# Rows turned by TensorE's transpose path, logits from stationary gate weights

## The chip, the cores and the metric

One core of one Trainium2 chip. The metric is the device time of one execution in microseconds (us). Of the kernel before there are three timed executions and one profiled one.

## The reference, cut to what matters

A block-wise linear attention (64-row blocks, decay `lam` per head) is followed by a mixture-of-experts layer in which each token goes to one expert.

```python
# q, k, v: (4, 8, 768, 64); attention output (B,H,S,D) -> x: (3072, 512)
x = attn_out.transpose(0, 2, 1, 3).reshape(B * S, H * D)
logits = x @ w_gate                      # (3072, 512) @ (512, 8)
expert_idx = np.argmax(logits, axis=1)
probs = softmax(logits)                  # gate_w = probs of the chosen expert
for e in range(8):
    mask = expert_idx == e
    h = np.maximum(x[mask] @ w1[e], 0.0) # w1: (8, 512, 1024)
    out[mask] = gate_w[mask, None] * (h @ w2[e])   # w2: (8, 1024, 512)
```

All data is fp32.

## The kernel before, in words

**Attention stage.** The work is cut into 12 steps (`order`): six blocks of 128 positions times two pairs of batches. A step is a struct `m` (`begin`). In the main loop, iteration i handles `cur` (step i), prepares `ahead` (step i+1), and finishes `last` (step i-1). TensorE, VectorE, ScalarE and SyncE follow the order in which the code is written. In an iteration TensorE does, in this order:

- the rows of `last` (`leave` calls `rows`): its attention output, which stands feature-major in SBUF (`xT`), is turned to token-major and multiplied by the gate weights;
- the turns of `ahead` (`turn_q`, `turn_k`: `tq`, `tk`, 16 transposes of 128x128);
- `attend_states(cur, 0)`: products with the running state, in 64x64 quadrants of the array (`op`, L306);
- `grow`: the state update (`cp`, L335); `attend` (`op`, L318); `attend_states(cur, 1)`; for every second step `put` (the `rank` products);
- `score(ahead)` (`sp`, L282), in two row halves of the array.

ScalarE copies what stands in PSUM: from `rows` the logits (`lg`, L364) and the rows (`x`, L366), then `qT`, `kT`, the exponential `ex`, a one-column copy `fence` (L314), and at the end of the iteration `xT` (L327). `fence` reads the last column that `attend_states(cur, 0)` wrote, and `attend` writes the same bank, so TensorE's L318 waits for `fence`. Since each engine works its queue in order, `fence` waits for whatever ScalarE has before it, `ex` included. `ex` waits for VectorE's `sh`.

VectorE multiplies scores by the decay (`mt`), makes `qsT` out of `tq` behind ScalarE's `qT`, and runs `choose` (argmax and one-hot: `mx`, `sh`, `key`, `pick`, `oh`, `ohc`). `choose` runs once per group of four batches, that is in iterations 2, 4, 6, 8 and 10, and for the last block once per pair (iteration 11 and after the loop).

In the kernel before, each turn in `rows` is a plain fp32 matmul: the moving operand `back` holds, per pair of 128-feature chunks, the identity and the gate columns side by side, 136 columns, so one product gives turned rows and logits at once. Odd chunks stand with their 64-feature halves exchanged (`out_at`), and `back` undoes that.

SyncE's queue holds, per iteration, the store of the last step's rows to DRAM (`store_rows`, `xs`) and the three loads of step i+3 (`load`: q, k, v, each 512 KB in 256-byte pieces). GpSimd scales k (`kd`) and scatters routing entries (`slots`).

**Expert stage.** `hidden(zero)`, `outputs`, then seven passes with a Strassen-like scheme (`form`, L689 and L711) over gathered tokens. `load_first` and `load_second` bring an expert's weights.

PSUM has eight banks, given by number: `tq`/`tk`/`sp` use 0 to 3, `cp` 4, `rank` 5, `op` 6 and 7, and the four `tx` tiles 4 to 7.

Of the kernel before, what the change touches and what calls it, by code (L numbers as in the profile page):

```python
# [22 lines left out]
def kernel(  # L23
# [99 lines left out]
    W = P + E  # L123
    back = const.tile([P, DC // 2, 2 * W], F32, name="back")
    for c in range(DC // 2):
        nc.gpsimd.tensor_copy(back[:, c, :P], ident)
        nc.gpsimd.tensor_copy(back[:, c, P + 2 * E:W + E + D], ident[:, D:])
        nc.gpsimd.tensor_copy(back[:, c, W + E + D:], ident[:, :D])
    by_chunk = moe_w_gate.rearrange("(c j u d) e -> j u d c e", c=DC // 2, j=2, u=2)
    for j, u in itertools.product(range(2), range(2)):  # L130
        nc.gpsimd.dma_start(out=back[(u ^ j) * D:((u ^ j) + 1) * D, :, P + j * E:P + (j + 1) * E],
                            in_=by_chunk[j, u])
# [54 lines left out]
    def load_first(e):  # L187
        w1t = wpool.tile([P, DC, F], F32, tag="w1", name="w1t")
        nc.sync.dma_start(out=w1t, in_=pick(w1_r, e))
        return w1t  # L190
# [19 lines left out]


# [112 lines left out]
    def to_sbuf(m):  # L324
        for b in range(2):
            xT = work.tile([P, DC, C], F32, tag="xT", name="xT")
            nc.scalar.copy(xT, m.op[b])  # L327
            m.xT.append(xT)
# [21 lines left out]
    def rows(m, b, lg):  # L350

        if b == 0:
            m.x = row_pair("x")
        x = m.x[:, b]
        tx = [bank(4 + 2 * b + c, [P, 2, W], f"tx{c}") for c in range(DC // 2)]
        for c, t in enumerate(tx):
            flat = t.rearrange("p j w -> p (j w)")
            nc.tensor.matmul(flat[:, :W], lhsT=m.xT[b][:, 2 * c, :], rhs=back[:, c, :W],  # L358
                                 start=True, stop=False, skip_group_check=True)
            nc.tensor.matmul(flat[:, P:P + W], lhsT=m.xT[b][:, 2 * c + 1, :],  # L360
                                 rhs=back[:, c, W:], start=False, stop=True,
                                 skip_group_check=True)
        for c, t in enumerate(tx):
            nc.scalar.copy(lg[:, c, :], t[:, 0, P:])  # L364

            nc.scalar.copy(x.rearrange("p (a d f) -> p d a f", a=P // Q, d=DC)[:, 2 * c:2 * c + 2],  # L366
                           t[:, :, :P].rearrange("p d (a f) -> p d a f", f=Q))
# [5 lines left out]
    def choose(n, bs, lg):  # L373
        nb = len(bs)
        shp = [P, nb, E]
        parts, lg = lg, small.tile(shp, F32, tag="lg_sum", name="lg_sum")
        nc.vector.tensor_add(lg, parts[:, :, 0], parts[:, :, 1])
# [35 lines left out]
    def put(n, bs, oh, ohc, sh):  # L413
# [4 lines left out]
        rank = bank(5, shp, "rank")  # L418
# [230 lines left out]
    def token_sums(m):  # L649
        b = [[m.xgT[:, j * DH:(j + 1) * DH, k, m.off[k]:m.off[k] + m.h] for k in range(2)] for j in range(2)]  # L650
        t1, t2, t4 = (work.tile([P, DH, m.h], F32, tag=t, name=f"t_{t}", bufs=n)
                      for t, n in (("sd", 2), ("xT", 2), ("kd", 2)))

        m.b = right_sums(b, t1, t2, b[0][1], t4, nc.vector.tensor_sub)
# [205 lines left out]
    def leave(m):  # L860
        for b in range(2):
            n, bs = group_of[m.n, m.b + b]
            i = bs.index(m.b + b)
            if i == 0:
                lgs[0] = small.tile([P, len(bs), DC // 2, E], F32, tag="lg", name="lg")
            rows(m, b, lgs[0][:, i])
        store_rows(m)
        if i == len(bs) - 1:
# [54 lines left out]
    with tc.manual_schedule(engines={mybir.EngineType.PE, mybir.EngineType.DVE,  # L923
# [9 lines left out]
        for i in range(len(order)):  # L933
# [8 lines left out]
            new = leave(last) if last else None  # L942
# [6 lines left out]
            else:  # L949
                later_decays()  # L950
            if new:
# [23 lines left out]
            if ahead:  # L975
                for s in range(2):
# [4 lines left out]
                  1)  # L981
# [121 lines left out]
```

## Time and profile before

| | us |
|---|---|
| median of 3 runs | 442.14 (441.17 to 448.15) |
| profiled execution, its own time | 445.17 |
| span of the profiled execution | 443.3 |
| TensorE matmul busy in the span | 424.9 (96%) |
| VectorE / ScalarE / GpSimd busy | 265.7 / 152.7 / 120.5 |

The mean granted TensorE clock was 0.991 of full speed. The attention stage takes roughly the first 131 us; the rest is the expert stage. In the rows below, PE is TensorE's matmuls, PEld its weight loads, DVE VectorE, ACT ScalarE, POOL GpSimd, SP SyncE. An fp32 matmul leaves two records (two passes), a transpose one, so "x2" at `tx` is one product and "x4" at `tq` four transposes.

### The profile page before, as it was taken

The numbers are of one execution on the slowest core, as the hardware profiler recorded it, in microseconds if no ns is written. First come the engines' busy times: TensorE is split into PE (matmuls) and PEld (weight loads), VectorE is DVE, ScalarE is ACT, GpSimd is POOL, SyncE is SP. The second block draws the span as 40 slices with busy tenths as digits, with TensorE's granted clock in tenths as the row PEclk, the third lists the DMA queues.
The fourth block names the chain that finished last, engine by engine and source line by source line (L and its number), as shares of the span: only waits on it lengthen the run. The fifth ranks groups of instructions, "written<-read, shape, count | busy, mean of one in ns | idle before, by whom it ended". The sixth has DMA issues, their size and how long they took to land.

```text
span 443.3 us, 9039 instructions
## 1 busy us (share of the span) xinstructions
PE 424.9 (96%) x3575; PEld 397.9 (90%) x3575; DVE 265.7 (60%) x567; ACT 152.7 (34%) x370; POOL 120.5 (27%) x140
## 2 busy tenths in 40 slices
PE   3999999989999999999999999999999999999993
PEld 3989999889888569999999999999999999999772
DVE  2846556555654146784688289479749839937411
ACT  2355544534561110441144135224414413413411
POOL 6425373605062540052104200600500200200121
PEclk9999999989999999999999999999999999999997
DMA  9999999999986989779979859947977966605012
GB/s 176 240 227 239 205 202 196 204 208 195 291 230 160 295 234 370 226 197 362 261 211 375 230 134 325 327 96 242 355 185 187 356 193 148 229 24 125 27 59 73
DMA packets 128208, 95.52 MB, mean 216 GB/s; under 512 B 81955, under 2 KB 104103, under 8 KB 128157
## 3 DMA queue, kind: packets, MB, share of 16 engines
q1 hardware_dynamic: 120813, 80.75, 70.9%
q0 software_dynamic: 5264, 13.58, 10.0%
q10 hardware_dynamic: 2080, 0.52, 0.6%
q8 instruction: 30, 0.49, 0.5%
q14 instruction: 21, 0.17, 0.1%
HBM read 70.41 MB, written 24.65 MB: 214 GB/s over the span
## 4 chain that ended last, share of the span: by engine, by line
PE 90%; SPq 3%; DMA 2%; DVE 1%; ACT 1%; issue 1%; POOLq 0%; POOL 0%; DVEq 0%
PE p L689 29%; PE p L711 25%; PE sp L282 5%; PE po L815 5%; PE ph L566 4%; PE op L318 4%; SPq L109 3%; PE p L787 3%; PE op L306 3%; PE tx L358 2%; PE cp L335 2%; DMA qkv_in<-in_k_dram 2%; PE tx L360 2%; PE tk L254 2%; PE tq L239 2%; PE po L731 2%
## 5 line engine op out<-in xcount | busy, mean ns | idle before, releaser
L523 POOL DMA_INDIRECT out_dram<-o,list x21 | 22.2, 1057 | 175.7 <-ACT o L775 171.2
L711 PE MATMUL p<-hT,w2t 128*128 128x204 f32 (+3 forms) x288 | 49.9, 330 | 0.0
L711 PEld LDWEIGHTS p<-hT,w2t 128*128 128x128 f32 x288 | 48.2, 190 | 0.0
L699 ACT ACTIVATE hT<-hT 128x408 f32<-128x408 f32 (+4 forms) x56 | 29.4, 527 | 48.2 <-DVE hT L698 48.1
L689 PE MATMUL p<-xgT,w1t 128*128 128x204 f32 (+4 forms) x224 | 39.1, 328 | 0.0
L689 PEld LDWEIGHTS p<-xgT,w1t 128*128 128x128 f32 x224 | 37.1, 190 | 0.0
L719 DVE TENSOR_TENSOR yT<-p,u_qsT 128x408 f32<-128x408 f32 (+3 forms) x18 | 10.2, 568 | 44.7 <-ACT u_qsT L605 29.2
L517 POOL DMA_INDIRECT xg<-xs,list x24 | 25.6, 1066 | 40.0 <-DMA ye<-yb 25.2
L288 DVE TENSOR_TENSOR mt<-sp,decay 128x512 f32<-128x512 f32 x48 | 29.9, 683 | 8.2 <-PE sp L282 8.2
L698 DVE TENSOR_TENSOR hT<-p,u_qsT 128x408 f32<-128x408 f32 (+4 forms) x42 | 23.4, 562 | 17.9 <-PE p L689 12.7
L282 PE MATMUL sp<-qT,kT 64*128 64x128 f32 x384 | 26.6, 291 | 2.2 <-issue 2.1
L282 PEld LDWEIGHTS sp<-qT,kT 64*128 64x128 f32 x384 | 24.4, 200 | 3.7 <-issue 2.9
L433 POOL DMA_INDIRECT slots<-entry,slot_i x24 | 23.3, 972 | 15.5 <-DVE slot_i L431 5.1
L592 ACT COPY u_qT<-p 128x408 f32<-128x408 f32 (+5 forms) x21 | 9.9, 473 | 45.4 <-PE p L689 39.1
L327 ACT COPY xT<-op 128x512 f32<-128x512 f32 x24 | 12.9, 589 | 36.4 <-PE op L306 26.1
L566 PE MATMUL ph<-xgT,w1t 128*128 128x256 f32 (+1 forms) x128 | 21.9, 330 | 0.5 <-DVE xgT L531 0.5
L566 PEld LDWEIGHTS ph<-xgT,w1t 128*128 128x128 f32 x128 | 19.5, 190 | 2.1 <-ACT xgT L529 0.6
L815 PE MATMUL po<-w2t,hT 128*128 128x512 f32 (+1 forms) x48 | 20.9, 592 | 0.0
L689 PE MATMUL p<-t_sd,w1t 128*128 128x204 f32 (+4 forms) x112 | 20.7, 328 | 0.0
L689 PE MATMUL p<-xgT,s_k 128*128 128x204 f32 (+4 forms) x112 | 20.7, 328 | 0.0
L689 PE MATMUL p<-t_xT,s_q 128*128 128x204 f32 (+4 forms) x112 | 20.7, 328 | 0.0
L689 PE MATMUL p<-t_kd,w1t 128*128 128x204 f32 (+4 forms) x112 | 20.7, 328 | 0.0
(190 smaller groups left out, 895.6 us busy)
## 6 DMA issues: line engine op xcount, KB each, us to landing
w1t<-in_moe_w_dram SPq DMA_DIRECT2D x8, 2048.0 KB, 12.8
w2t<-in_moe_w_dram SPq DMA_DIRECT2D x8, 2048.0 KB, 11.1
xs<-x SPq DMA_DIRECT2D x12, 512.0 KB, 7.9
xe<-xg SPq DMA_DIRECT2D x7, 512.0 KB, 8.6
q_in<-in_q_dram SPq DMA_DIRECT2D x6, 512.0 KB, 7.1
k_in<-in_k_dram SPq DMA_DIRECT2D x6, 512.0 KB, 9.7
v_in<-in_v_dram SPq DMA_DIRECT2D x6, 512.0 KB
y<-ye SPq DMA_DIRECT2D x6, 512.0 KB, 3.7
```

What stands on the lines that cost most here:

```text
L282: nc.tensor.matmul(sp[u][:, i, b, :], lhsT=m.kT[s][halves[u], i, b, :], rhs=m.qT[s][halves[u], i, b, :], start=(i == 0 and b == 0), stop=( ...
L288: nc.vector.tensor_mul(mt[:, u], sp[u], decay[:, u, s * HP // 2:(s + 1) * HP // 2].unsqueeze(2).to_broadcast(shp))
L318: nc.tensor.matmul(out_at(m, b, u, hp), lhsT=m.v[:, b, 2 * hp + u, :], rhs=m.mt[hp // 2][:, u, hp % 2, b, :], start=(m.n == 0 and hp == 0) ...
L433: in_line(nc.gpsimd.indirect_dma_start(out=slots, out_offset=bass.IndirectOffsetOnAxis(ap=slot_i[:, i:i + 1], axis=0), in_=entry[:, n, b, ...
L517: in_line(nc.gpsimd.indirect_dma_start(out=dst, out_offset=None, in_=xs[:rows, :], in_offset=bass.IndirectOffsetOnAxis(ap=idx, axis=0)))
L523: in_line(nc.gpsimd.indirect_dma_start(out=out, out_offset=bass.IndirectOffsetOnAxis(ap=idx, axis=0), in_=src, in_offset=None, bounds_chec ...
L566: nc.tensor.matmul(ph, lhsT=w1t[:, dc, fc * P:(fc + 1) * P], rhs=m.xgT[:, dc, 0, :m.h], start=(dc == 0), stop=(dc == DC - 1))
L689: nc.tensor.matmul(p[:, i, :], lhsT=lhs[:, dc, (c + i) * P:(c + i + 1) * P], rhs=rhs[:, dc, :], start=(first and i == 0 and dc == 0), stop ...
L698: nc.vector.tensor_add(outs[i][k], p, u)
L699: nc.scalar.activation(outs[i][k], outs[i][k], ACT.Relu)
L711: nc.tensor.matmul(p[:, i, :], lhsT=rhs[:, fc, i * P:(i + 1) * P], rhs=lhs[:, fc, :], start=(first and i == 0 and fc == 0), stop=(end and ...
L815: nc.tensor.matmul(po[part], lhsT=m.hT[:, fc, t * P:t * P + w], rhs=w2t[:, fc, :], start=(i < k), stop=(i >= FC - k), skip_group_check=True)
```

## The change

The rows are turned by plain transposes against the identity, eight of 128x128 per step, in two PSUM tiles (banks 4 and 7). The logits come from four products in which the gate weights (128x32, zero behind the eighth column) are stationary and `xT` moves, 256 columns each; the four go to four 32-partition strips of bank 5. They are partial sums, one per 128-feature chunk. ScalarE copies them to SBUF (`lt`), TensorE turns them back by two transposes (`sum_logits`), and one VectorE reduction adds the four parts. `leave` (the back turn, the reduction and `choose`) now stands behind the turns of `ahead`. The exchanged halves of odd chunks are no longer undone in the rows: the rows keep that order, and `load_first` brings w1's rows in the same order, in three DMAs in place of one. `xT` becomes one tile for both batches, single-buffered; bank 5 is one tile (`five`) for partial logits, their turn and `rank`.

```diff
-    W = P + E
-    back = const.tile([P, DC // 2, 2 * W], F32, name="back")
...
+    gate = const.tile([P, DC, Q], F32, name="gate")
+    nc.gpsimd.memset(gate, 0.0)
...
     def load_first(e):
         w1t = wpool.tile([P, DC, F], F32, tag="w1", name="w1t")
-        nc.sync.dma_start(out=w1t, in_=pick(w1_r, e))
+        src = pick(w1_r, e)
+        for j, h in ((0, slice(0, P)), (1, slice(0, D)), (1, slice(D, P))):
+            fr = slice(0, P) if j == 0 else slice(D - h.start, P + D - h.stop)
+            nc.sync.dma_start(out=w1t[h, j::2], in_=src[fr, j::2])
...
-    def rows(m, b, lg):
...
-            nc.tensor.matmul(flat[:, :W], lhsT=m.xT[b][:, 2 * c, :], rhs=back[:, c, :W],
-                                 start=True, stop=False, skip_group_check=True)
-            nc.tensor.matmul(flat[:, P:P + W], lhsT=m.xT[b][:, 2 * c + 1, :],
...
+    def logits(m):
+        lt = five[:, :2 * C].rearrange("p (b c) -> p b c", b=2)
+        for c in range(DC):
+            nc.tensor.matmul(lt[c * Q:(c + 1) * Q], lhsT=gate[:, c, :], rhs=m.xT[:, :, c, :],
+                             start=True, stop=True, skip_group_check=True)
+        m.lt = small.tile([P, 2, C], F32, tag="lt", name="lt", bufs=1)
+        nc.scalar.copy(m.lt, lt)
+
+    def rows(m):
+        m.x = row_pair("x")
+        for b in range(2):
+            tx = bank((4, 7)[b], [P, DC, C], "tx")
+            for c in range(DC):
+                nc.tensor.transpose(tx[:, c, :], m.xT[:, b, c, :], ident)
+            nc.scalar.copy(m.x[:, b].rearrange("p (a d f) -> p d a f", a=P // Q, d=DC),
+                           tx.rearrange("p d (a f) -> p d a f", f=Q))
+
+    def sum_logits(m, lg):
+        back = five[:, :2 * C].rearrange("p (b c) -> p b c", b=2)
+        for b in range(2):
+            nc.tensor.transpose(back[:, b], m.lt[:, b, :], ident)
+        nc.vector.reduce_sum(lg, back.rearrange("p b (c e) -> p b e c", e=Q)[:, :, :E], axis=AX.X)
...
-            new = leave(last) if last else None
+            if last:
+                logits(last)
+                rows(last)
+                store_rows(last)
             if i + AT_ONCE < len(order):
                 load(i + AT_ONCE)
...
+            new = leave(last) if last else None
             if new:
                 weigh(*new)
             attend_states(cur, 0)
...
         turn_rows(passes[0], (0, 1), lambda shp: ffn.tile(shp, F32, tag="xgT", name="xgT", bufs=1),
-                  1)
+                  1, lambda t: t or logits(last))
+        rows(last)
+        store_rows(last)
         new = leave(last)
```

The built program shows what moved. First TensorE's queue in an iteration, between the scores of the step ahead and the first products with the state; before:

```order
L282 MATMUL sp_654<-qT,kT 128x128
L358 MATMUL tx_668<-back,xT 128x136
L360 MATMUL tx_668<-back,xT 128x136
L358 MATMUL tx_669<-back,xT 128x136
L360 MATMUL tx_669<-back,xT 128x136
L358 MATMUL tx_678<-back,xT 128x136
L360 MATMUL tx_678<-back,xT 128x136
L358 MATMUL tx_679<-back,xT 128x136
L360 MATMUL tx_679<-back,xT 128x136
L239 MATMUL tq<-ident,q_in 128x128 x4
L254 MATMUL tk<-ident,k_in 128x128 x4
```

The same place on TensorE now (line numbers are those of the changed file):

```order
L284 MATMUL sp_646<-qT,kT 128x128
L354 MATMUL five<-xT,gate 32x256 x4
L364 MATMUL tx<-ident,xT 128x128 x8
L241 MATMUL tq<-ident,q_in 128x128 x4
L256 MATMUL tk<-ident,k_in 128x128 x4
L241 MATMUL tq<-ident,q_in 128x128 x4
L256 MATMUL tk<-ident,k_in 128x128 x4
L371 MATMUL five<-ident,lt 128x128 x2
L308 MATMUL op_720<-qsT,st 64x128
```

Eight products of 136 columns have become four strips of 256 columns, eight transposes, and two more behind the turns. Second, VectorE's queue in an iteration that chooses, from the last score product on; before, the choice stands ahead of `qsT`:

```order
L288 TENSOR_TENSOR mt<-sp_804,decay 128x512
L377 TENSOR_TENSOR lg_sum<-lg 128x32
L379 TENSOR_REDUCE mx<-lg_sum 128x4
L381 TENSOR_TENSOR sh<-lg_sum,mx 128x32
L384 SCALAR_TENSOR_TENSOR key<-sh,rev 128x32
L388 TENSOR_REDUCE pick<-key 128x4
L394 TENSOR_TENSOR oh<-key,pick 128x32
L397 COPY ohc<-ohc 128x8
L399 TENSOR_TENSOR ohc<-ohc,oh 128x8 x4
L245 TENSOR_TENSOR qsT<-tq,qdec 128x512 x2
```

The same place on VectorE now, where both `qsT` come first and the reduction of the back-turned parts behind them:

```order
L290 TENSOR_TENSOR mt<-sp_796,decay 128x512
L247 TENSOR_TENSOR qsT<-tq,qdec 128x512 x2
L372 TENSOR_REDUCE lg<-five 128x16
L382 TENSOR_REDUCE mx<-lg 128x4
L384 TENSOR_TENSOR sh<-lg,mx 128x32
L387 SCALAR_TENSOR_TENSOR key<-sh,rev 128x32
L391 TENSOR_REDUCE pick<-key 128x4
```

So `sh`, for which ScalarE's `ex` waits, has moved behind the second `qsT`. Third, ScalarE's queue in such an iteration, where now two wide copies of rows and one of partial logits stand in place of eight small ones, with `ex` and `fence` at the end as before:

```order
L357 COPY lt<-five 128x256
L365 COPY x<-tx 128x4x4x32 x2
L243 COPY qT<-tq 128x512
L258 COPY kT<-tk 128x512
L243 COPY qT<-tq 128x512
L258 COPY kT<-tk 128x512
L410 ACTIVATE ex<-sh 128x32
L316 COPY fence<-op_890 64x1
```

Of eight copies ahead of the first `qT`, three are left; the rest of this queue kept its order.

More of the change, by code (lines that the diff above doesn't have):

```diff
@@ L120 @@
     make_identity(nc, ident)
-    W = P + E
-    back = const.tile([P, DC // 2, 2 * W], F32, name="back")
[L125 to L132, printed above, removed]
+    gate = const.tile([P, DC, Q], F32, name="gate")
+    nc.gpsimd.memset(gate, 0.0)
+    by_chunk = moe_w_gate.rearrange("(c j h p) e -> j h p c e", c=DC // 2, j=2, h=2)
+    for j in range(2):
+        for h in range(2):
+            nc.gpsimd.dma_start(out=gate[h * D:(h + 1) * D].rearrange(
+                "p (c j) e -> p j c e", j=2)[:, j, :, :E], in_=by_chunk[j, h ^ j])
     before = const.tile([P, P], BF16, name="before")
@@ L208, in bank @@
         return ps.tile(shape, F32, tag=f"bank{i}", name=name)
+    five = bank(5, [P, 4 * C], "five")
     st = once.tile([P, B, HP, D], F32, tag="h2", name="st")
@@ L324, in to_sbuf @@
     def to_sbuf(m):
+        m.xT = work.tile([P, 2, DC, C], F32, tag="xT", name="xT", bufs=1)
         for b in range(2):
-            xT = work.tile([P, DC, C], F32, tag="xT", name="xT")
-            nc.scalar.copy(xT, m.op[b])
-            m.xT.append(xT)
+            nc.scalar.copy(m.xT[:, b], m.op[b])
     def grow(m):
@@ L375, in choose @@
         shp = [P, nb, E]
-        parts, lg = lg, small.tile(shp, F32, tag="lg_sum", name="lg_sum")
-        nc.vector.tensor_add(lg, parts[:, :, 0], parts[:, :, 1])
         mx = small.tile([P, nb, 1], F32, tag="mx", name="mx")
@@ L417, in put @@
         shp = list(oh.shape)
-        rank = bank(5, shp, "rank")
+        rank = five[:, 3 * C:3 * C + shp[1] * E].rearrange("p (b e) -> p b e", e=E)
         for lhs, rhs in ((before, oh), (ones, ohc[:, :shp[1]])):
@@ L651, in token_sums @@
         t1, t2, t4 = (work.tile([P, DH, m.h], F32, tag=t, name=f"t_{t}", bufs=n)
-                      for t, n in (("sd", 2), ("xT", 2), ("kd", 2)))
+                      for t, n in (("sd", 2), ("xT", 1), ("kd", 2)))
         m.b = right_sums(b, t1, t2, b[0][1], t4, nc.vector.tensor_sub)
@@ L860, in leave @@
     def leave(m):
[L861 to L868, printed above, removed]
+        n, bs = group_of[m.n, m.b]
+        i = bs.index(m.b)
+        if i == 0:
+            lgs[0] = small.tile([P, len(bs), E], F32, tag="lg", name="lg")
+        sum_logits(m, lgs[0][:, i:i + 2])
+        if i + 2 == len(bs):
             return choose(n, bs, lgs[0])
```

12 lines of the change are left out of this document (removed).

## The prediction

> **What bounds the kernel now.** I read the page's engine shares and slices first, to see which engine fills the attention stage:
>
> ```profile
> PE 424.9 (96%) x3575; PEld 397.9 (90%) x3575; DVE 265.7 (60%) x567; ACT 152.7 (34%) x370; POOL 120.5 (27%) x140
> PEclk9999999989999999999999999999999999999997
> DMA  9999999999986989779979859947977966605012
> ```
>
> TensorE is busy 96% of the span, at full clock but for two slices, the last among them; the DMA engines are as full as TensorE through the first twelve slices, the attention stage. The busy time by stretch says the same of one whole stretch:
>
> ```profile
> 40.00:60.00 20.00, 20.00 (x328) 18.26 (x326) 12.29 (x33) 9.96 (x31) 10.20 (x11) 1.00 1.12 226
> ```
>
> TensorE has no gap, VectorE and ScalarE half or less. So what is cut from TensorE here shortens the stage, unless a wait or the loads take it back. The chain of waits gives the pieces of one iteration (start, duration, then how many records):
>
> ```profile
> 69.91 0.43 PE tx L358 x2
> 70.33 0.23 PE tx L360 x2
> ...
> 71.96 0.44 PE tq L239 x4
> ...
> 74.46 1.08 PE cp L335 x32
> 75.54 1.75 PE op L318 x32
> 77.29 0.60 PE op L306 x16
> ...
> 133.88 12.19 PE ph L566 x56
> ```
>
> The rows take 71.96 - 69.91 = 2.05 us: eight products, the first 0.43, the others 0.23. The first is 0.20 dearer, since TensorE comes from the half-array tiles of `sp`. A transpose costs 0.44/4 = 0.11, half of a product of about its size. A pass of 256 columns costs 12.19/56 = 0.218. In L306 eight products in four quadrants need 0.60: two passes of 0.11 for two groups of four are 0.44, so four run abreast and the entry costs 0.16. In L318, sixteen products in two column halves need 1.75 = 16 x 0.11: two abreast.
>
> **The loads.** SyncE's queue in the same stage:
>
> ```profile
> 93.27 0.46 SPq L109 DMA_DIRECT2D q_in<-in_q_dram  x1
> 93.82 3.16 SPq L109 DMA_DIRECT2D k_in<-in_k_dram  x1
> 97.08 2.25 SPq L109 DMA_DIRECT2D v_in<-in_v_dram  x1
> 99.42 3.71 SPq L371 DMA_DIRECT2D xs<-x  x1
> ...
> 103.88 2.54 SPq L109 DMA_DIRECT2D k_in<-in_k_dram  x1
> DMA to landing us min/median/max: 8.2/9.7/12.0
> 115.69 0.60 PE L254 MATMUL tk<-ident,k_in 128*128 128x128 f32 x4
> 24.06 0.63 PE L254 MATMUL tk<-ident,qkv_in 128*128 128x128 f32 x4 [0.87 <-DMA qkv_in<-in_k_dram]
> ```
>
> The issues stand end to end: the queue is held back by the transfers, not by TensorE. The landing line is `k_in`'s. The last k, issued at 103.88, lands near 113.6 by the median, and TensorE uses it at 115.69: some 2 us of slack (0 at the longest landing). In iteration 1 TensorE waits 0.87 for k already. So what TensorE gains before the last turns is worth about 2 us at most.
>
> **The change, part by part.** *TensorE per iteration.* Added: four strips of 256 columns. No row shows four column strips; from L306 I take four abreast, 2 x 0.218 = 0.44, and its entry of 0.16. Bounds: 0.44 with no entry, and 4 x 0.44 = 1.75 one after another. Eight transposes, 0.88, entered from strips: 0.20 as at `tx` (bounds 0 and 0.20). Two back turns, 0.22. Sum 0.60 + 0.20 + 0.88 + 0.22 = 1.90 against 2.05: **0.15 less** (bounds: 0.51 less; 1.16 more). The back turns wait for `lt`, which ScalarE finishes about 1 us before the turns of q and k end; it costs nothing.
>
> [...] L306 shows four abreast, but quadrants; of full-height strips the trace shows only L318's two, at the ideal.
>
> *The fence.* This is what I expect to be late next. ScalarE and VectorE in the choosing iteration above, and two `qsT` from the one before:
>
> ```profile
> 72.48 0.59 ACT L241 COPY qT<-tq 128x512 f32<-128x512 f32 x1
> 72.99 0.59 ACT L256 COPY kT<-tk 128x512 f32<-128x512 f32 x1
> 73.47 0.59 ACT L241 COPY qT<-tq 128x512 f32<-128x512 f32 x1
> 74.43 0.25 ACT L407 ACTIVATE ex<-sh 128x32 f32<-128x32 f32 x1
> 74.56 0.15 ACT L314 COPY fence<-op 64x1 f32<-64x1 f32 x1
> 72.19 0.19 DVE L377 TENSOR_TENSOR lg_sum<-lg 128x32 f32<-128x32 f32 x1 [0.66 <-ACT lg L364]
> 72.64 0.19 DVE L381 TENSOR_TENSOR sh<-lg_sum,mx 128x32 f32<-128x32 f32 x1
> 63.64 0.60 ACT L241 COPY qT<-tq 128x512 f32<-128x512 f32 x1
> 64.27 0.69 DVE L245 TENSOR_TENSOR qsT<-tq,qdec 128x512 f32<-128x512 f32 x1 [0.29 <-ACT qT L241]
> ```
>
> Before, `sh` is done at 72.83, 1.6 us before `ex` needs it, and `fence` ends at 74.71, well ahead of L318 at 75.54. Now count from the start of the rows, 69.91 here. The first half of the rows is ready at 0.60 + 0.20 + 0.44 = 1.24; wide copies follow each other every 0.49 (72.48 to 73.47 are two), so rows start at 1.27 and 1.76, `qT`, `kT`, `qT`, `kT` at 2.25, 2.74, 3.23, 3.72. The second `qsT` starts 0.63 behind its `qT`, at 3.86, and holds VectorE for 0.69; the reduction starts at 4.55, and 0.45 later, as from 72.19 to 72.64, comes `sh`, done at 5.19. `ex` follows at 5.22, `fence` ends 0.28 behind the start of `ex` (74.43 to 74.71), at 5.50, and L318 can go on at 5.55. TensorE without the wait would be there at 75.54 - 69.91 - 0.15 = 5.48. So choosing iterations gain 5.63 - 5.55 = 0.08 instead of 0.15, and 0.08 is all they gain however quick TensorE becomes. For the reduction over four parts I take a small VectorE operation's 0.19; twice that delays L318 by 0.19.
>
> Iteration 10 has no `cp` (1.08) to cover this:
>
> ```profile
> 113.37 0.43 PE tx L358 x2
> ...
> 117.69 2.25 PE L318 MATMUL op<-mt,v_in 128*64 128x128 f32 x32
> 118.19 1.51 PEld L318 LDWEIGHTS op<-mt,v_in 128*64 128x64 f32 x28 [0.30 <-ACT fence L314]
> ...
> 122.67 0.43 PE tx L358 x2
> ...
> 126.23 1.51 PEld L318 LDWEIGHTS op<-mt,v_in 128*64 128x64 f32 x28 [0.19 <-ACT fence L314]
> ```
>
> Its rows start at 113.37, and L318 goes on at 118.19, 4.82 behind them; at 5.55 it is **0.73 later**. Queued behind L318 are the second L306, `rank` and all later scores. Iteration 11 has no turns: rows end at 1.68, back turns at 1.90, L306 waits for the second row copy (1.76 + 0.6), the fence ends at about 3.2, against 126.23 - 122.67 = 3.56 before: 0.33 earlier. After the loop the same sum without the turns leaves about 0.1.
>
> *The rest.* SyncE: `store_rows` keeps its place ahead of the loads, so the queue that is held back does not move. One w1 load becomes three:
>
> ```profile
> w1t<-in_moe_w_dram SPq DMA_DIRECT2D x8, 2048.0 KB, 12.8
> ...
> 216.31 19.32 PE p L689 x112
> ```
>
> That is two more issues of about 0.4 (as q's 0.46), and the same bytes. The cover is the double-buffered weights: the first half of one expert's pass alone (L689) takes 19.32 on TensorE, against 12.8 to land. If that cover failed, 0.8 per expert, 5.6 in all. GpSimd's start: a memset for six copies, under the first load. Single-buffered `xT`: its readers are done early in the iteration, its next writer comes at the end. ScalarE loses five copies per iteration and had time to spare.
>
> **The sum.** Iteration 1 gives its part to the load (0). Iterations 3, 5, 7, 9: 4 x 0.15 = 0.60. Iterations 2, 4, 6, 8: 4 x 0.08 = 0.32. Iteration 10: -0.73. Iteration 11 and the end: 0.43. Together **0.6 us less**, under the 2 us of slack. The profiled execution, 445.17 with a span of 443.3, would become 444.6. It holds a stall which the median need not have:
>
> ```profile
> 22.19:25.60 3.41, 2.54 (x24) 2.17 (x24) 0.74 (x2) 2.41 (x8) 0.00 (x0) 1.00 1.25 219
> 87.05:90.46 3.41, 1.30 (x29) 1.12 (x27) 0.69 (x1) 1.07 (x2) 1.16 (x2) 1.00 1.40 161
> 90.46:93.87 3.41, 3.41 (x30) 3.19 (x29) 2.04 (x4) 0.00 (x0) 0.00 (x0) 0.50 0.86 178
> ...
> 22.19:25.60 3.41, 1.20 (x8) 0.94 (x8) 0.69 (x1) 0.92 (x2) 1.00 1.25 219
> ...
> 22.19:25.60 3.41, 1.23 (x8) 0.89 (x8) 0.59 (x1) 1.00 1.25 219
> ```
>
> The first three rows are all work, the last two only `tq` and `tk`. TensorE idles 2.1 us before 90.46 and then runs 3.41 us at half clock: some 3.8 us, where 445.17 lies 3.0 above 442.14. From the median I get 442.14 - 0.6 = 441.5, and forecast **441.5**.
>
> **The rivals.** *1, a clean gain (0.19).* Entries cost nothing and the choice is quicker than I count: nine iterations of up to 0.51 and no loss in iteration 10 exceed the slack, so the loads cap it at about 2, and iteration 11 and the end add 0.4: 439.7. For: ScalarE and VectorE are half idle. Against: the entry costs in the rows.
>
> *2, the loads take it all (0.14).* Landing 12.0 instead of 9.7 leaves no slack: 442.1.
>
> *3, two strips at a time, as L318 (0.11).* 0.44 more in twelve rounds, 5.3, less 0.6: 446.8.
>
> *4, strips one after another (0.04).* 4 x 0.44 = 1.75 instead of 0.44 in twelve rounds is 15.7 more, less 0.6: 457.2, **slower**. It passes 2% of slowdown where strips take over 0.44 + (8.8 + 0.6)/12 = 1.22. Against it: no tiled product in the trace runs singly.
>
> *5, half clock (0.04).* An iteration now has 8 + 16 + 2 transposes, 2.9 us, nearly one of those 3.41-us stretches. If transposes did not count as work, each iteration could be followed by a stretch at half clock, 1.7 us lost, in ten iterations 17, less 0.6: 458.5. Against: the stretch from 22.19 to 25.60 held little but transposes (1.20 + 1.23 of 2.54 busy) and stayed at 1.00, as did what followed; the half clock came behind 1.30 busy of 3.41. [...]
>
> **How the numbers follow.** My forecast has 0.48; the rivals have the chances given. The range runs from rival 1 less 1 us, 438.5, to just above rival 3, 447.5; rivals 4 and 5 stay out. About 2% (8.8 us) is what a measurement of this kernel tells from no change: same 0.90, slower 0.08 (rivals 4 and 5), faster 0.02, since no case reaches 433.
>
> **What would show it.** `five<-xT,gate`: four strips starting together, about 0.6 us for the lot (1.75 would be rival 4). `tx`: eight times 0.11. PE L320 waiting for ACT's fence in iteration 10, by about 1.3 us (118.19 - 117.69 and 0.73), and hardly in the others; DVE's reduction directly behind the second `qsT`. SyncE's issues as dense as before. I am wrong if the first `tk` of iterations begins to wait for k by more than 1 us in total, if PEclk shows dips in the attention slices, or if the expert stage, from the first `p`, differs in length by over 1 us.

## The result: slower, at the end of the attention stage

| | before | after |
|---|---|---|
| time, median (range) | 441.77 us (441.17 to 448.15, 4 runs) | 450.21 us (449.82 to 451.36, 4 runs) |
| ratio, 95% interval | | 1.0145 [1.0099, 1.0191] |
| profiled execution, span | 445.17, 443.3 | 449.82, 447.6 |

The forecast was 441.5 with a range to 447.5; the change costs 8.4 us. At 1.45% it stays under the 2% that the prediction set for "slower", so its "same" came out, but by luck: the time moved the other way and by more than the range allows. (The chip of this pair isn't on record. The experiments below fell on four chips: on one, called of the first kind, the kernel before takes 444 us, on three, of the second kind, 451 to 453, and each run is compared with the kernel before on its own chip. Medians are of all runs; ratios leave out runs more than 1.5% above the fastest of their kernel.)

The page after, engine shares and the row of the granted clock:

```profile
PE 422.3 (94%) x3599; PEld 389.1 (87%) x3599; DVE 274.0 (61%) x572; ACT 149.4 (33%) x310; POOL 118.3 (26%) x135
PEclk9999999999979999999999999999999999999997
```

TensorE works 2.6 us less than before (422.3 against 424.9) in a span that is 4.3 longer, so the loss is waiting. PEclk dips in the twelfth slice, 123 to 134 us, the end of the attention stage; such a dip was one of the prediction's signs of being wrong. From the steady `ph` on, nothing changed: 133.88 to the end before, 138.20 now, and 138.20 - 133.88 is the 4.3 of the span. Before held a stall of 3.8 which the changed kernel's profile does not; without it the difference is 8.1, near the 8.4 of the medians.

Starts of the rows, iteration by iteration, place these 8.1 us (iterations of before that hold the stall are left out):

| piece | before | after | difference | forecast |
|---|---|---|---|---|
| to the first rows | 20.64 | 19.21 | -1.4 | 0 |
| iteration 1 | 9.67 | 8.37 | -1.3 | 0 |
| 3, 5, 7, 9 (do not choose), each | 9.81 | 9.57 | -0.24 | -0.15 |
| 2, 4, 6 (choose), each | 9.96 | 10.78 | +0.82 | -0.08 |
| 8 (chooses) | 9.96 | 10.98 | +1.0 | -0.08 |
| 10 | 9.30 | 9.88 | +0.6 | +0.73 |
| from the rows of 11 to the steady `ph` | 11.3 | 19.1 | +7.9 | -0.43 |

TensorE in one choosing iteration after (start, duration, what; in brackets the idle time ahead of it and what ended it):

```profile
47.93 0.64 PE L354 MATMUL five<-xT,gate 128*32 128x256 f32 x8
48.50 1.09 PE L364 MATMUL tx<-ident,xT 128*128 128x128 f32 x8
...
51.18 0.38 PE L371 MATMUL five<-ident,lt 128*128 128x128 f32 x2
...
55.68 0.19 PE L423 MATMUL five<-oh,before 128*128 128x32 bf16 x1
56.62 0.18 PE L423 MATMUL five<-ohc,ones 128*128 128x32 bf16 x1 [0.76 <-DVE ohc L402]
```

The strips need 0.57 up to the first transpose, the eight transposes 0.93. But the second half of `rank`, off the count in the forecast, now waits 0.76 for VectorE's `ohc` (3.2 us in the four choosing iterations, the longest 0.9). VectorE and GpSimd beside it:

```profile
52.85 0.19 DVE L384 TENSOR_TENSOR sh<-lg,mx 128x32 f32<-128x32 f32 x1
53.08 0.93 DVE L387 SCALAR_TENSOR_TENSOR key<-sh,rev 128x32 f32<-128x32 f32 x1
54.04 0.19 DVE L391 TENSOR_REDUCE pick<-key 128x4 f32<-128x32 f32 x1
54.27 0.74 DVE L397 TENSOR_TENSOR oh<-key,pick 128x32 bf16<-128x32 f32 x1
54.93 1.05 DVE L400 COPY ohc<-ohc 128x8 bf16<-128x8 bf16 x1
52.92 2.04 POOL L267 TENSOR_TENSOR kd<-k_in,kdec 128x512 f32<-128x512 f32 x2 [6.28 <-PE cp L336]
54.92 1.04 POOL L276 TENSOR_TENSOR sd<-st,sdec 128x512 f32<-128x512 f32 x1
```

The same steps in iteration 10, where GpSimd has no such products:

```profile
114.33 0.19 DVE L387 SCALAR_TENSOR_TENSOR key<-sh,rev 128x32 f32<-128x32 f32 x1
114.77 0.19 DVE L397 TENSOR_TENSOR oh<-key,pick 128x32 bf16<-128x32 f32 x1
114.88 0.16 DVE L400 COPY ohc<-ohc 128x8 bf16<-128x8 bf16 x1
```

`key` ends at 54.01, `oh` at 55.01, `ohc` at 55.98: each within 0.05 us of the end of one of GpSimd's three products (53.96, 54.96, 55.96). `pick`, a reduction in the same stretch, takes its 0.19. So the choice was moved into the 3 us in which GpSimd scales k and the state.

Then the end of the stage, after: TensorE, ScalarE, SyncE's queue, GpSimd, and the median time from issue to landing of the two gathers:

```profile
126.91 0.66 PE L560 MATMUL tr<-ident,xo 128*128 128x128 f32 x4 [1.99 <-ACT xo L552]
132.22 1.08 PE L354 MATMUL five<-xT,gate 128*32 128x256 f32 x8 [4.65 <-ACT xT L329]
126.23 0.62 ACT L552 COPY xo<-xg 128x512 f32<-128x512 f32 x1 [3.86 <-DMA xg<-xs,list_0a]
130.57 0.62 ACT L552 COPY xo<-xg 128x512 f32<-128x512 f32 x1 [3.72 <-DMA xg<-xs,list_0a]
105.74 3.04 SPq L189 DMA_DIRECT2D w1t<-in_moe_w_dram  x3
112.58 0.78 POOL L471 DMA_DIRECT2D list_0a<-slots  x1 [8.09 <-DMA xs<-x]
121.79 0.99 POOL L520 DMA_INDIRECT xg<-xs,list_0a  x1 [8.42 <-DMA xs<-x]
121.84 1.53 SPq L194 DMA_DIRECT2D w2t<-in_moe_w_dram  x1
xg<-xs,list_0a POOLq DMA_INDIRECT x2, 5.9
```

The list of the first tokens is issued 6.8 us behind w1's 2 MB, the gathers 9.2 later; the second of the gathered blocks is there at 130.57; ScalarE copies in order, so `xT` (L329, at 131.10), the logits and the rows stand behind it. (The brackets of the list and the gather name `xs`, which came last; the list reads what the last put writes, and the gather reads the list.) TensorE idles 6.6 us, and the granted clock is half for 6.83 us, in which it works 3.39 (rows of the stretches, with granted clock third from the right):

```profile
104.00:128.78 24.78, 20.55 (x332) 16.73 (x328) 12.92 (x47) 8.37 (x20) 6.74 (x8) 1.00 0.88 236
128.78:135.61 6.83, 3.39 (x19) 2.58 (x20) 0.00 (x0) 3.41 (x7) 2.33 (x3) 0.50 0.46 167
```

Before, TensorE waited for nothing there; the list, the gathers, w1 and w2:

```profile
113.14 0.46 SPq L189 DMA_DIRECT2D w1t<-in_moe_w_dram  x1
114.44 0.78 POOL L468 DMA_DIRECT2D list_0a<-slots  x1 [6.27 <-DMA slots<-entry,slot_i]
121.92 1.02 POOL L517 DMA_INDIRECT xg<-xs,list_0a  x1 [6.70 <-ACT xT L327]
125.65 0.47 SPq L194 DMA_DIRECT2D w2t<-in_moe_w_dram  x1
126.46 1.28 ACT L549 COPY xo<-xg 128x512 f32<-128x512 f32 x2 [0.28 <-DMA xg<-xs,list_0a]
xg<-xs,list_0a POOLq DMA_INDIRECT x2, 4.2
```

w1 was issued 1.3 us ahead of the list, not 6.8, and the list took 7.5 us to the gather, not 9.2. Two more things differ. The gathers were issued at the same time as now (121.92 and 121.79), but TensorE now comes to the rows of iteration 11 at 119.06 instead of 122.60: it is earlier and they are not. And w2 was issued behind both gathers; now it is issued ahead of the second one (123.09), which takes 7.5 us until its copy can start. So a gather behind w2 is a second suspect beside the list behind w1. One reservation: this profile before holds the stall, which gave the gathers 3.8 us more; that the kernel waits for nothing without it is read from its median alone.

### The profile page after: what moved, and what is told of

Read it like the earlier page. It is cut to its first block, busy times and chain, and to the rows that moved or that the text cites. A ratio compares the mean times of both kernels' runs of the same rounds, so it can differ in the third digit from the quotient of the medians.

```text
span 447.6 us, 9065 instructions
## 1 busy us (share of the span) xinstructions
PE 422.3 (94%) x3599; PEld 389.1 (87%) x3599; DVE 274.0 (61%) x572; ACT 149.4 (33%) x310; POOL 118.3 (26%) x135
## 4 chain that ended last, share of the span: by engine, by line
PE 69%; DVE 0%; POOLq 0%; ACT 0%; POOL 0%; issue 0%; DVEq 0%
PE p L692 29%; PE p L714 25%; PE ph L569 5%; PE po L818 5%; PE p L790 3%; PE po L734 2%; PE tx L364 0%; PE tr L560 0%; PE five L354 0%; POOLq L1062 0%; DVE xgT L534 0%; DVE o L800 0%; ACT xT L329 0%; POOL out_dram L526 0%; PE five L371 0%
## 5 line engine op out<-in xcount | busy, mean ns | idle before, releaser
L722 DVE TENSOR_TENSOR yT<-p,u_qsT 128x408 f32<-128x408 f32 (+3 forms) x18 | 10.2, 568 | 44.7 <-ACT u_qsT L608 29.1
L520 POOL DMA_INDIRECT xg<-xs,list x24 | 24.6, 1026 | 44.0 <-DMA list<-slots 26.1
L284 PEld LDWEIGHTS sp<-qT,kT 64*128 64x128 f32 x384 | 22.4, 188 | 5.4 <-PE five L423 2.8
L284 PE MATMUL sp<-qT,kT 64*128 64x128 f32 x384 | 24.8, 279 | 0.0
L329 ACT COPY xT<-op 128x512 f32<-128x512 f32 x24 | 12.9, 588 | 32.4 <-PE op L308 25.6
L569 PE MATMUL ph<-xgT,w1t 128*128 128x256 f32 (+1 forms) x128 | 21.9, 331 | 0.5 <-DVE xgT L534 0.5
L247 DVE TENSOR_TENSOR qsT<-tq,qdec 128x512 f32<-128x512 f32 x20 | 13.8, 692 | 11.8 <-ACT qT L243 11.8
## 6 DMA issues: line engine op xcount, KB each, us to landing
w2t<-in_moe_w_dram SPq DMA_DIRECT2D x8, 2048.0 KB, 10.5
```

The lines of the kernel that those rows point to most:

```text
L247: nc.vector.tensor_mul(qsT, tq, qdec[:, s * HP // 2:(s + 1) * HP // 2].unsqueeze(2).to_broadcast(shp))
L284: nc.tensor.matmul(sp[u][:, i, b, :], lhsT=m.kT[s][halves[u], i, b, :], rhs=m.qT[s][halves[u], i, b, :], start=(i == 0 and b == 0), stop=( ...
L520: in_line(nc.gpsimd.indirect_dma_start(out=dst, out_offset=None, in_=xs[:rows, :], in_offset=bass.IndirectOffsetOnAxis(ap=idx, axis=0)))
L569: nc.tensor.matmul(ph, lhsT=w1t[:, dc, fc * P:(fc + 1) * P], rhs=m.xgT[:, dc, 0, :m.h], start=(dc == 0), stop=(dc == DC - 1))
```

## The experiments

**First reading: the split load, or w2.** Two suspects were tried first: w1 in three parts, and w2 ahead of the gathers' data. On this chip the kernel before takes 452.5 us.

The kernel before, unchanged:

> The kernel before once more, for a trace without the stall near 88 us. If the stall (about 3.8 us) is what lifts the first profiled execution over the median, this one takes 441 to 442 us, its rows of iteration 11 start near 119 us instead of 122.6, and both early gathers land before TensorE wants them. If the median runs hold the stall too, the span stays near 443.

Measured 451.66, span 449.8. On such a chip the iterations that do not choose take about 11 us instead of 9.6 to 9.8 in every kernel run there, with idle time in `cp` for which the profile names no releaser, and the kernel before itself waits at the end of the stage, though not for the gathers. The trace without the stall that this run was to give is thus not there: on the chip of the loss none is on record. The rows of `b_again`:

```profile
46.03 0.82 PE L335 MATMUL cp<-qkv_in,kd 128*64 128x64 f32 x21 [0.52 <-issue]
...
127.43 1.01 PE L306 MATMUL op<-qsT,st 64*64 64x128 f32 x16 [1.53 <-PE tx L360]
131.64 3.25 PE L318 MATMUL op<-mt,v_in 128*64 128x128 f32 x28 [2.84 <-ACT fence L314]
```

The changed kernel with w1 in one load (its rows then do not stand in the order of x's columns):

```diff
-        src = pick(w1_r, e)
-        for j, h in ((0, slice(0, P)), (1, slice(0, D)), (1, slice(D, P))):
-            fr = slice(0, P) if j == 0 else slice(D - h.start, P + D - h.stop)
-            nc.sync.dma_start(out=w1t[h, j::2], in_=src[fr, j::2])
+        nc.sync.dma_start(out=w1t, in_=pick(w1_r, e))
```

> The changed kernel with w1 loaded in one DMA, as before (w1's rows then do not stand in the order of x's features). Theory A (the three-part load is slower in flight, 12.9 us instead of 8.9, and holds up the list and the early gathers behind it): the early gather's second half lands 4 us earlier or more, TensorE's waits of 2.0 and 4.65 us at the end of the attention stage go, 443 to 446 us. Rival B (SyncE gets ahead and the w2 load passes the gathers, whatever form w1's load has): stays at 449 to 451.

Measured 452.02 (449.57 to 454.55, 10 runs), 0.9995 [0.9967, 1.0023]; choosing iterations 10.78, gathers at 121.95 and 123.25. The kernel before with w1 in three parts:

```diff
-        nc.sync.dma_start(out=w1t, in_=pick(w1_r, e))
+        src = pick(w1_r, e)
+        for j, h in ((0, slice(0, P)), (1, slice(0, D)), (1, slice(D, P))):
+            nc.sync.dma_start(out=w1t[h, j::2], in_=src[h, j::2])
```

> The kernel before with w1 loaded in the three parts of the change (rows in natural order). Theory A: the first w1 load takes 12 to 13 us in flight instead of 8.9 and the early gathers come late: 445 to 449 us. Rival B: within 1.5 us of before, since nothing gets ahead on SyncE.

Measured 452.82, 1.0011 [0.9982, 1.0039]. The changed kernel with w2 behind the second gather on SyncE's queue:

```diff
+        probe = dram.tile([1, ENTRY], F32, name="probe")
+        nc.sync.dma_start(out=probe, in_=passes[0].xg[0:1, 1, 0:ENTRY])
         w2t = load_second(0)
```

> The changed kernel with one small DMA ahead of the first w2 load in SyncE's queue that reads a row of the second early gather, so that the w2 load is issued only when that gather has landed. Rival B: the second gather lands near 126.5 us instead of 130.5, the half clock goes with the wait: 443 to 446 us. Theory A: the gathers come little earlier, since w1 holds up the list: 448 to 451 us.

Measured 454.35, 1.0041 [1.0013, 1.0068]. Neither the split nor w2 moves the time by the size of the loss here. That doesn't settle them where the loss shows: with the split undone, or with w2 held back, the copies `xo` wait for no gather, and with the split undone SyncE comes to w2 only at 128.23, 5 us behind the second gather, so on such a chip w2 was not in front to begin with. With the split added to the kernel before, the profile does have the list 8.8 us ahead of the gather (6.5 unchanged) and a wait of 5.63 for the second block (w2 is issued 0.2 us behind its gather), but that execution, 454.6, is the slowest of ten, and the median does not move. (In flight, w1 took 11.4 us before and its parts 11.9 to 14.2 after; the 8.9 of the expectations is not what the traces show.) In the corners below the split stays and most of the loss goes, so the split alone is not the loss. w2's place was not tried again.

**Second reading: the held copy, and w1 ahead of the list.** On a chip on which the kernel before takes 452.14; first the changed kernel as it is.

> The changed kernel as it is, once more, beside the kernel before on the same chip, as the base for the next three. If the loss belongs to the kernel: again 1.010 to 1.019 of the time before. If it belongs to the chip on which it was first seen (on a second chip the kernel before itself took 452.5 and lost in iterations that do not choose what the change loses in those that do): 0.995 to 1.005.

Measured 453.12 (10 runs), 1.0023 [0.9992, 1.0054]: where the kernel before waits at the end as well, the loss does not show. (The wait here is a different one: ScalarE stands idle for 6.96 us ahead of `lt`, with no releaser named, and the copies `xo` wait for no gather.) The copy:

```diff
-        nc.vector.tensor_copy(ohc[:, 0], so_far[0])
+        nc.vector.tensor_tensor(out=ohc[:, 0], in0=so_far[0], in1=so_far[0], op=ALU.max)
```

> One edit to the changed kernel: the copy of 8 bf16 values that begins the running counts (ohc) becomes a VectorE operation with two inputs (the maximum of the counts and themselves). Theory 1 (the copy is held until GpSimd has ended kd and sd, and rank waits for it): ohc's first step takes 0.15 to 0.3 instead of 1.05, TensorE's wait of 0.75 ahead of rank goes, choosing iterations fall from 10.78 to between 9.9 and 10.2, about 3 us over four of them up to the last rows. Of the time, 0 to 3 us less than the changed kernel, since the first gathers at the end wait for a list and not for TensorE. Rival (the VectorE chain behind the second qsT is simply late, whatever the operation): the pitch stays at 10.7 to 10.8.

A miss: 453.34, 1.0030 [0.9992, 1.0068], pitch 10.77 as before, and the new operation is held like the copy:

```profile
56.71 1.05 DVE L400 TENSOR_TENSOR ohc<-ohc 128x8 bf16<-128x8 bf16 x1
```

It is not the copy alone that is held; from here on the theory is that each of `key`, `oh` and the first `ohc` waits. Then w1:

```diff
-            if i == len(order) - 3:
+            if i == len(order) - 2:
                 w1t = load_first(0)
```

> One edit to the changed kernel: the first load of w1 is issued one iteration later (at the third but one place before, now the second but one), behind one more store of rows. Theory 2 (the 2 MB of w1 now stand in the queues ahead of the early puts, the list that reads them and the store of rows, and these hold up the early gathers): the two gathers issue by 114 to 118 us instead of 121.8, the second xo copy stands before 127 instead of at 130.6, TensorE has no wait of 4.65 ahead of the last logits, and the time falls by 3 to 6 us against the changed kernel. Rival (the gathers are late because of the split of the load or because of w2's): gathers and xo where they were, or w1 now lands behind the first ph and the time grows by up to 4 us.

Measured 450.98 (449.68 to 451.8), 0.9976 [0.9954, 0.9998], 2.1 less than the changed kernel beside it, not the 3 to 6 expected. The gathers issue at 118.44 and 119.74 instead of 122.4 and 123.7, later than expected, and the steady `ph` starts at 139.6 instead of 142.5. Both edits:

> Both edits together. If theories 1 and 2 both hold, the gains add, since the end then follows TensorE: 5 to 9 us less than the changed kernel, 0.98 to 0.995 of the time before. If only one holds, the time of that one alone.

450.07, 0.9963 [0.9938, 0.9989]: 3.05 less; since the first edit does nothing by itself, the range of 5 to 9 was missed.

**Third reading: the place of the choice.** On a third chip (before: 451.22). The choice back ahead of the turns:

```diff
             if last:
                 logits(last)
                 rows(last)
                 store_rows(last)
+            new = leave(last) if last else None
...
-            new = leave(last) if last else None
             if new:
                 weigh(*new)
```

> One edit to the changed kernel: back turns, reduction and choice stand directly behind the store of rows again, ahead of the turns of q and k, so that VectorE has done the choice before GpSimd begins kd and sd. Theory 1b (three VectorE operations of the choice, key, oh and the first ohc, each wait for the end of one of GpSimd's three products; iteration 10, which has none of these, has them at 0.19, 0.19 and 0.16): key, oh and ohc take 0.16 to 0.2 in all choosing iterations, rank's wait of 0.75 and the fence's wait of 0.87 in iteration 10 go, choosing iterations take 9.7 to 10.0 instead of 10.78. About 3 to 5 us less up to the last rows; of the time 0 to 3 less than the changed kernel, as long as the early gathers are late. Rival (the choice is as slow wherever it stands, or TensorE now waits for the partial logits in the back turns): the pitch stays above 10.5.

Choosing iterations take 9.71, as expected, and all three operations their own time (`oh` 0.19):

```profile
51.22 0.19 DVE L387 SCALAR_TENSOR_TENSOR key<-sh,rev 128x32 f32<-128x32 f32 x1
...
51.78 0.16 DVE L400 COPY ohc<-ohc 128x8 bf16<-128x8 bf16 x1
```

The time was 449.56, 0.9972 [0.9935, 1.0009], not clear of no change. Then the move alone, in the kernel before:

```diff
-            return choose(n, bs, lgs[0])
+            return n, bs, lgs[0]
...
+            new = new and choose(*new)
             if new:
                 weigh(*new)
...
-        new = leave(last)
+        new = choose(*leave(last))
```

> The kernel before with one part of the change alone: the choice on VectorE (sum of logits and all behind it) moved behind the turns of q and k; rows and logits are as before. Theory 1b: key, oh and ohc are held by kd and sd as in the changed kernel, rank waits 0.7 to 1.3, choosing iterations take 10.6 to 11.3 instead of 9.95; 3 to 5 us more up to the last rows, of the time 0 to 4. Rival (the loss belongs to the strips or to the shared PSUM bank): choosing iterations stay at 9.9 to 10.1.

457.8 (456.87 to 458.53, 4 runs), 1.0151 [1.0087, 1.0216]: without the quicker rows the move costs 1.5% by itself; the whole change on a like chip had a ratio of 1.0023, not clear of 1. Choosing iterations take 11.12. The wait is not at `rank`, as expected, but at the fence, since here even `sh` is held, and `ex` and the fence stand behind it:

```profile
57.95 1.02 DVE L381 TENSOR_TENSOR sh<-lg_sum,mx 128x32 f32<-128x32 f32 x1
57.89 2.04 POOL L265 TENSOR_TENSOR kd<-k_in,kdec 128x512 f32<-128x512 f32 x2 [6.75 <-issue]
59.33 1.75 PE L318 MATMUL op<-mt,v_in 128*64 128x128 f32 x28 [0.90 <-ACT fence L314]
```

The late w1 load in the kernel before (edit as above):

> The kernel before with the first w1 load issued one iteration later. Theory 2 (2 MB of w1 ahead of the early puts, their list and the rows hold up the early gathers, and TensorE waits at the end of the stage as soon as the rest is early or the transfers slow): the gathers issue 3 to 7 us earlier, the wait at the end of the stage goes, the time falls by 2 to 5 us. Rival (only the changed kernel has this problem, by its split load): no difference.

449.42, 0.9943 [0.9912, 0.9974]: it helps there too, by 1.8 us, just under the range. Choice first and w1 late, both edits as above:

> The changed kernel with the choice ahead of the turns and the first w1 load one iteration later. If theories 1b and 2 hold, both losses go: choosing iterations at 9.7 to 10.0, no wait at the end of the stage, 445 to 449 where the kernel before takes 452, 0.983 to 0.993. If the loads set the pace of the iterations instead, the time of the late load alone, 0.9976.

447.55 (445.32 to 450.53), 0.9919 [0.9885, 0.9954], the largest gain, though under 2%. The wait at the end, which was to go, is not gone: the second copy `xo` still waits 2.08 for its gather.

**How long a hold lasts.** On a chip of the first kind (before: 444.45). GpSimd's products in halves:

```diff
-                in_line(nc.gpsimd.tensor_tensor(
-                    out=kd, in0=m.k[:, :, hs],
-                    in1=kdec[:, hs].unsqueeze(1).unsqueeze(3).to_broadcast(shp), op=ALU.mult))
+                for b in range(2):
+                    in_line(nc.gpsimd.tensor_tensor(
+                        out=kd[:, b], in0=m.k[:, b, hs],
+                        in1=kdec[:, hs].unsqueeze(2).to_broadcast([P, HP, D]), op=ALU.mult))
```

and the state's product likewise.

> One edit to the changed kernel: GpSimd scales k and the state in six instructions of 128x256 instead of three of 128x512; the same work. If a VectorE operation waits for the end of the GpSimd instruction that runs (an exclusive hold, instruction by instruction), key, oh and the first ohc take at most 0.2 + 0.5 each instead of 0.93, 0.74 and 1.05, the choice ends 1.0 to 1.6 earlier, rank's wait of 0.75 goes, choosing iterations take 9.9 to 10.2 instead of 10.78. Rival (the two engines share, and VectorE is slow as long as GpSimd works): the three last as long together as before, about 2.7, and the pitch stays.

```profile
53.07 0.51 DVE L389 SCALAR_TENSOR_TENSOR key<-sh,rev 128x32 f32<-128x32 f32 x1
53.83 0.32 DVE L399 TENSOR_TENSOR oh<-key,pick 128x32 bf16<-128x32 f32 x1
54.07 0.63 DVE L402 COPY ohc<-ohc 128x8 bf16<-128x8 bf16 x1
54.73 1.86 DVE L404 TENSOR_TENSOR ohc<-ohc,oh 128x8 bf16<-128x8 bf16 x4
```

The holds shrink with GpSimd's instruction, to about half: `key`, `oh` and `ohc` end at 53.58, 54.15 and 54.70, while GpSimd's six products, 0.58 and 0.60 us each by the mean, run from 52.92 to 56.39. So here a VectorE operation waited for the end of the product that ran, not for GpSimd's work as a whole. The pitch was missed (10.62, not 9.9 to 10.2): the adds behind `ohc` now fall into the same stretch and are held in turn (1.86 for the four instead of 0.75). The times fall into two groups, three of 442.1 to 442.4 and seven of 448.5 to 450.7 (ratio 1.0017 [0.9939, 1.0094]). The profiled execution, 442.34, is of the first group and has no wait at the end of the stage beyond 0.6, though its choice is late and its w1 early. There w1 was issued 10.9 us ahead of the list (101.91 and 112.83), the list took 5.9 us to the gather, w2 was issued behind both gathers, and the first copy `xo` starts 4.3 us behind its gather. So w1 ahead of the list, by those 10.9 us, did no harm there. None of the seven was traced, so what sets the groups apart is open.

w1 behind the gathers, in the version with both edits:

```diff
+                probe = dram.tile([1, ENTRY], F32, name="probe")
+                nc.sync.dma_start(out=probe, in_=passes[0].xg[0:1, 1, 0:ENTRY])
+                w1t = load_first(0)
```

> The best so far (choice ahead of the turns, late w1 load) with the first w1 load behind a read of 12 bytes of the second early gather on the same queue, so that w1 can't pass the gathers. If what is left of the wait at the end of the stage is w1 still ahead of the gathers' data (the second xo copy stood at 128.46, 12 us behind its gather's issue): both xo copies right behind the fence, no wait between them, first steady ph 1 to 3 us earlier, 0.986 to 0.991 of the time before. Rival: w1 now lands too late and ph waits for it, 0.99 to 1.0.

The rival, and worse than it: 447.45, 1.0078 [1.0036, 1.0120]. Nothing holds the gathers, the first `ph` starts at 123.6, and then waits for w1, issued at 114.37:

```profile
128.42 2.90 PE L569 MATMUL ph<-xgT,w1t 128*128 128x256 f32 x6 [4.13 <-DMA w1t<-in_moe_w_dram]
```

**Four corners on one chip** (before: 444.2 us, 24 runs), to read the two effects against each other.

> The changed kernel unchanged, as one corner of four that share a chip (choice late or first, w1 early or late). On a chip on which the kernel before takes 441 to 445: 449 to 451, 1.010 to 1.018. On one on which it takes 451 to 453: 1.000 to 1.005.

> The corner with the choice ahead of the turns and the early w1 load. Choosing iterations 9.7, as seen before. If the loss of the changed kernel sits in the choosing iterations, 3 to 5 us less than the changed kernel; if it sits at the end of the stage, where the gathers stand behind w1, 0 to 2 less.

> The corner with the late choice and the late w1 load. If the loss sits at the end of the stage: 4 to 8 us less than the changed kernel where that takes 449 to 451, with no wait of 4.65 for xT ahead of the last strips and at most one stretch of 3.4 us at half clock. If in the choosing iterations: 0 to 2 less.

> The corner with the choice first and the late w1 load. If the two losses add, the sum of the two other corners' gains, within 1.5 us: 0.975 to 0.99 of the time before on a chip of the first kind (its w1 is issued some 6 us earlier than behind the guard, by 108, and lands by 122, ahead of the first ph), about 0.992 on one of the second kind. If w1 lands too late, as behind the guard, 1.00 or more.

| choice, w1 | time (median) | ratio to before | choosing iteration | last put, list, first gather issued | w1 issued | steady `ph` from |
|---|---|---|---|---|---|---|
| late, early: the changed kernel | 450.54 | 1.0166 [1.0129, 1.0202] | 10.78 | 103.97, 114.31, 123.39 | 109.85 | 139.1 |
| first, early | 443.45 | 0.9994 [0.9959, 1.0030] | 9.72 | 100.95, 109.03, 116.47 | 109.14 | 130.3 |
| late, late | 445.85 | 1.0025 [0.9983, 1.0066] | 10.78 | 103.95, 111.07, 115.25 | 112.39 | 135.6 |
| first, late | 442.14 | 0.9957 [0.9917, 0.9998] | 9.72 | 99.25, 105.89, 109.76 | 107.86 | 130.1 |

GpSimd's queue (and SyncE's w1) of the first corner, then of the second:

```profile
103.97 0.97 POOL L436 DMA_INDIRECT slots<-entry,slot_i  x1 [0.30 <-issue]
109.85 1.99 SPq L189 DMA_DIRECT2D w1t<-in_moe_w_dram  x3
114.31 0.79 POOL L471 DMA_DIRECT2D list_0a<-slots  x1 [9.36 <-DMA xs<-x]
123.39 1.00 POOL L520 DMA_INDIRECT xg<-xs,list_0a  x1 [8.30 <-DMA xs<-x]
```

```profile
100.95 0.97 POOL L436 DMA_INDIRECT slots<-entry,slot_i  x1 [0.31 <-issue]
109.03 0.79 POOL L471 DMA_DIRECT2D list_0a<-slots  x1 [7.11 <-DMA slots<-entry,slot_i]
109.14 2.22 SPq L189 DMA_DIRECT2D w1t<-in_moe_w_dram  x3
116.47 0.99 POOL L520 DMA_INDIRECT xg<-xs,list_0a  x1 [6.65 <-DMA list_0a<-slots]
```

In the first the list is issued 4.5 us behind w1, in the second just ahead of it. By the landing times in the first trace, the last put has landed at 114.0, the list at 122.6 and the last part of w1 at 122.8: the 4 KB come in with the 2 MB. From the last put to the first gather: 19.4, 15.5, 11.3, 10.5 us down the table. Either edit alone gives back more than half of the 8.4 us that both give (7.1 and 4.7), so the two losses do not add, as I had expected of them (11.8; 0.975 to 0.99 of the time before); they meet in one chain. The late choice makes the early puts late, late puts make the list late, and a late list stands behind w1. The second corner reaches the rows of iteration 11 only 3.3 us earlier than the first (116.23 against 119.50), and gains 7.1, which neither of its two expectations had. The times of the stage are of one profiled execution per corner. In these traces the gathers themselves take longer where weights are issued just ahead of them: from issue to landing (medians of the two) 4.2 us in the profile before, 7.3 in the first corner, with w2 issued 1.1 us ahead of them, and 10.2 in the third, with w1 2.9 us ahead. That fits the late w1 gaining only 4.7: TensorE still waits 3.03 for `xT`, which was expected to go, and meets 6.83 us of half clock, expected to be 3.4 at most. In the last corner the second gathered block also waits behind w1, and w1 behind the gathers comes too late, as shown above: the steady `ph` starts at 130 at the earliest, though TensorE comes to the rows of iteration 11 at 114.14.

## Why the prediction was wrong, step by step

- *TensorE per iteration*: right in kind, 0.24 less instead of 0.15. Four strips run abreast (0.57 with the entry, forecast 0.60), and the transposes take 0.11 each, with an entry of 0.05 instead of 0.20. In the trace the second pass of the four strips starts 0.24 behind the first, where one strip alone would need 0.218 by the pass of `ph`: four in 0.24 are 3.6 times as fast as one after another.
- *Rival 5* (half clock): its premise, that transposes do not count as work, is shown by no run. With ten iterations of 26 transposes each the clock was granted in full (1.00) up to 128.78; the half clock came behind a stretch, 125.36 to 128.78, in which TensorE worked 0.66 of 3.42 us, with the wait of 1.99 ahead of `tr`.
- *The fence*: right. Iteration 10 waits 0.87 for it and loses 0.6 (forecast 0.73); in the others it hardly waits.
- *The moved choice*: **the step that failed first.** I followed the choice to `sh`, `ex` and the fence and stopped. The rest of its chain, `key`, `oh` and `ohc`, leads to `rank`, and I let it run at the 0.19 of the old place without asking what else runs at the new one. Price: +0.82 to +1.0 instead of -0.08 in each of four iterations, about 3.5 us, shown by moving the choice back (9.71), by moving it alone (11.12), and by the halves. The profile before had a hint that I passed over, the first row in a choosing iteration, the second in iteration 10, without GpSimd's products:

```profile
55.93 0.43 DVE L410 TENSOR_SCALAR sm<-sm 128x4 f32<-128x4 f32 x1
119.16 0.17 DVE L410 TENSOR_SCALAR sm<-sm 128x4 f32<-128x4 f32 x1
```

- The trace after has what I missed row by row: beside GpSimd's products `key` takes 0.93, `oh` 0.74 and `ohc` 1.05, where iteration 10, without them, has 0.19, 0.19 and 0.16; `pick`, between them, keeps its 0.19. Why the reduction is not held and the others are was not tried.
- *Iteration 11 and the end*: **the step that cost most.** I gave it 0.43 of gain, from TensorE's instructions alone, and never laid the chain of early puts, list, gathers, `xo`, `xT` beside it, though all its rows stood in the profile. It is released by transfers. I had read SyncE's queue only as far as the last k, and treated w1 as bytes to be covered by the expert pass; its issue time against the small transfers was not a term. Measured: +7.9, with 6.6 of TensorE idle and 3.39 of work at half clock. How much of it is w2 ahead of the second gather, and not w1 ahead of the list, is open.
- *SyncE, "the queue that is held back does not move"*: wrong, and it feeds the step above. The queue moved up at once: the first store of rows is issued at 25.12 instead of 29.38, the sixth at 74.16 instead of 79.05, both ahead of the stall, and w1 at 105.74 instead of 113.14. The last early put, which the late choice holds, only went from 107.21 to 103.52, about the 3.8 of the stall. So w1 went from 1.3 to 6.8 us ahead of the list. Why the queue moved was not tried; it is not only held by transfers, as I had read: SyncE's stores wait 21.9 us for ScalarE's rows (four waits, the longest 8.9) in the profile before.
- *Rival 2* (the loads take it all) named the right kind of bound at the wrong place: not the last k, but w1 and the gathers at the end. With both losses mended TensorE reaches the rows of iteration 11 at 114.1 instead of 118.8 (122.60 less the stall), and the time gains 0.4%.
- *The split w1 load at nothing*: right for the expert stage, which is unchanged. For the first load it was tried only on a chip without the loss (1.0011).
- The 1.4 us up to the first rows and the 1.3 of iteration 1 I had at nothing. GpSimd's start is as much shorter (its first `kd` begins at 9.99 instead of 11.41); whether that is the cause was not tried.

Left open: w2's share of the loss at the end, on a chip that has the loss; why iterations that do not choose take about 11 us on some chips, and with that how much of the change shows there. In the last corner, how much of the floor at 130 is w1 and how much the stores beside it.

## What to carry to other kernels

When a piece of work is moved, lay every operation of it beside what the other engines do at the new place, VectorE beside GpSimd above all, and follow it to all its readers, not only to the nearest one. Look for operations of one line that last several times as long in some iterations, as `sm` (0.43 against 0.17) and `ohc` (1.05 against 0.16) did here: that was a hold, and it stood in the duration, not in the idle time. A small transfer on which a stage ends belongs into the sum with what is queued ahead of it (here the list: 9.1 us to its gather with w1 4.5 us ahead); a change that makes an engine faster can change who is first in the queues, as here w1 went from 1.3 to 6.8 us ahead of the list.

## What the runs showed of the hardware

- VectorE's `sh`, `key`, `oh` and first `ohc` (as a copy and as a maximum) were held to the end of GpSimd's running product: up to 1.05 us for an operation of 0.16, 0.63 with products of half the size; the reduction `pick` beside them was not (0.19).
- Four 32-column strips of 256 columns ran abreast in 0.57 us, the second pass 0.24 behind the first.
- From the issue of a list of 4 KB to that of the gather that reads it went 3.9, 4.2 and 7.4 us where w1 was issued 2.0, 1.3 and 0.1 us behind it, and 7.5, 9.1, 9.2 and 5.9 us where 2 MB of w1 were issued 1.3, 4.5, 6.8 and 10.9 us ahead (the four corners, the halves, the profiles before and after).
- The two gathers of the early tokens landed 4.2 us behind their issue with w1 issued 8.8 us ahead and w2 behind them, 7.3 with 2 MB of w2 issued 1.1 us ahead, 10.2 with w1 2.9 us ahead (medians of the two).
- The same kernel took 442 us in the first measurement, 444 on one chip and 451 to 453 on three others (medians).
